# Attention chunks of 32 tokens on eight TensorE tiles, instead of 64 tokens on four, in an RWKV-6 and MLP-mixer kernel

## The chip, the cores and the metric

The kernel runs on one core of a Trainium2 chip. The metric is device time in microseconds (us), the median of several executions. The span that a profile shows is some 2 us shorter than the device time of the same execution; the kernel before was profiled in an execution of 687.6 us, at the fast end of its times. PE is TensorE, DVE is VectorE, ACT is ScalarE. Intervals of ratios are 95%; behind a median stand the lowest and the highest time.

## The reference, cut to what matters

```python
# attention, batch 4, 8 heads, 768 tokens, head size 48, fp32
for t in range(S):
    cur = einsum('bhd,bhe->bhde', u * k[t], v[t])
    y[t] = einsum('bhd,bhde->bhe', r[t], state + cur)
    state = w[t][..., None] * state + einsum('bhd,bhe->bhde', k[t], v[t])
# then, on x = y laid out as (batch, 768, 384): token mixing, channel mixing
u = x + (relu(x.T @ w_tok1) @ w_tok2).T
out = u + relu(u @ w_ch1) @ w_ch2
```

The four mixing weights arrive in a 64-bit form and are converted on the chip, in 28 pieces.

## The kernel before

The recurrence is computed in chunks. A *unit* is 256 tokens of one batch for all heads; three units make a batch, twelve the problem. Inside a chunk of `T = 64` tokens the products of r and k are built level by level: at level l, blocks of 2^l tokens are joined, so 64 tokens need a first block and levels 1 to 5 (`LEVELS = 6` in all). Each level is a *gram* on PE, a masked copy of its result out of PSUM, where PE's results lie in this kernel, on DVE (for the upper levels a plain copy on ACT), and a scaling of k and r by decay products on DVE.

```python
def gram(l):                       # 8 pieces x 4 tiles = 32 fp32 matmuls
    ...
    for ca in range(UC * A):
        fours(lambda q, j, rows, cols: pe.matmul(
            g[cols, q, ts(ca, 32)], k_[rows, ds(ca * 128 + j * T, T)],
            right[rows, ts(2 * ca + j, 32 // b), :], start=True, stop=True))

def block(l):
    gram(l)
    join(l, products[l], products[l + 1])      # DVE: scales k and r, next decay product
    pick(l)                                    # DVE or ACT: masked copy out of PSUM

def carry(c):                      # k^T v of each chunk, then the state, chunk by chunk
    ...
        dve.tensor_mul(new, state[bt, g], L["w"][:, c, :, j].unsqueeze(2).to_broadcast([128, A, D]))
        dve.tensor_add(new, new, got)

def before(c): ...                 # y  = r @ state      (PE, tile row q, tile column j)
def within(c):                     # y += at @ v         (PE)
    ...
            pe.matmul(y[ts(j, T), q, ts(a, D)], at[ts(j, T), q, c * A + a, :],
                      vt[ts(j, T), c, ts(2 * a + q, D)], ...)   # tile row j, column j: the diagonal
```

The program is emitted in an order that weaves lists of pieces by weight; the compiler's scheduler then reorders inside what the dependences allow. Batch 0 has no mixing work to weave with its attention: its units 0 to 2 form the head of the program, together with the weight conversions. The attention of batch n+1 is woven with the mixing of batch n.

```python
emit(woven(levels(0), levels(1)))
emit(woven(levels(2), p0 + p1, to_tok1))           # p0, p1: the rest of units 0 and 1
...                                                # conversions woven with batch 0's mixing
emit(woven(att, pieces))                           # batch n+1's attention with batch n's mixing
```

## Time and profile before

| | before |
|---|---|
| median of 4 executions | 692.76 us (689.45 to 696.67) |
| span of the profiled execution | 685.6 us |
| PE instructions (a load or a matmul each) | 17,168 |
| first "back" matmul (second half of token mixing) of batches 0 to 3 | 85.3, 268.0, 423.0, 575.9 us |
| last weight conversion ends | 183.9 us |

The row of "back" matmuls is the ruler: they split a span into the head (to 85.3), batch 0's mixing with batch 1's attention (182.7), two dense batches (155.0 and 152.9) and the tail (109.7). The five sum to the span.

### The profile page before, as it was taken

The numbers are of one execution on the slowest core, as the hardware profiler recorded it, in microseconds if no ns is written. First come the engines' busy times: TensorE is split into PE (matmuls) and PEld (weight loads), VectorE is DVE, ScalarE is ACT, GpSimd is POOL, SyncE is SP. The second block draws the span as 40 slices with busy tenths as digits, with TensorE's granted clock in tenths as the row PEclk, the third lists the DMA queues.
The fourth block names the chain that finished last, engine by engine and source line by source line (L and its number), as shares of the span: only waits on it lengthen the run. The fifth ranks groups of instructions, "written<-read, shape, count | busy, mean of one in ns | idle before, by whom it ended". The sixth has DMA issues, their size and how long they took to land.

```text
span 685.6 us, 18835 instructions
## 1 busy us (share of the span) xinstructions
PE 641.6 (94%) x8584; PEld 466.9 (68%) x8584; DVE 293.1 (43%) x585; ACT 194.8 (28%) x489; POOL 7.2 (1%) x32
## 2 busy tenths in 40 slices
PE   3889998996799999999999999999999999999998
PEld 3877656863586666788677656788677655786854
DVE  5998899998821435442242305442132211000000
ACT  7144533441242123432321303432211201220200
POOL 3000000000000000000000000000000000000000
PEclk9997898998899999999999999999999999999999
DMA  9244544332202131110210312000000000000000
GB/s 345 69 107 132 146 140 126 124 115 71 70 25 81 36 95 48 25 25 5 80 35 3 94 35 60 2 2 2 13 13 2 25 12 12 1 0 12 12 16 31
DMA packets 16111, 38.56 MB, mean 56 GB/s; under 512 B 2176, under 2 KB 8320, under 8 KB 16032
## 3 DMA queue, kind: packets, MB, share of 16 engines
q1 hardware_dynamic: 15888, 37.36, 17.9%
q8 instruction: 67, 1.10, 0.7%
q14 instruction: 12, 0.10, 0.0%
q10 hardware_dynamic: 144, 0.00, 0.0%
HBM read 32.64 MB, written 4.72 MB: 54 GB/s over the span
## 4 chain that ended last, share of the span: by engine, by line
PE 87%; DVE 9%; issue 2%; ACT 1%; DMA 1%; SPq 0%; DVEq 0%; ACTq 0%
PE z_ps L375 29%; PE h_ps L384 28%; PE gram L225 9%; PE h_ps L353 5%; PE h_ps L360 5%; PE y_ps L331 4%; PE kv_ps L296 2%; PE y_ps L318 2%; DVE r L251 1%; DVE k L250 1%; PE kT_ps L284 1%; PE gram L211 1%; PE xT_ps L367 1%; DVE at L217 1%; DMA w<-in_rkw_dram 1%
## 5 line engine op out<-in xcount | busy, mean ns | idle before, releaser
L375 PE MATMUL z_ps<-xT,wch 128*128 128x256 f32 x864 | 203.2, 389 | 3.5 <-DVE wch L161 3.0
L384 PE MATMUL h_ps<-wch,z 128*128 128x384 f32 x576 | 198.6, 498 | 3.7 <-DVE wch L161 3.5
L375 PEld LDWEIGHTS z_ps<-xT,wch 128*128 128x128 f32 x864 | 161.4, 192 | 28.4 <-DVE wch L161 3.2
L384 PEld LDWEIGHTS h_ps<-wch,z 128*128 128x128 f32 x576 | 107.9, 192 | 73.1 <-DVE wch L161 3.7
L377 ACT ACTIVATE z<-z_ps 128x256 f32<-128x256 f32 x144 | 55.1, 383 | 177.3 <-PE z_ps L375 177.2
L225 PEld LDWEIGHTS gram<-r,k 48*64 48x64 f32 x3840 | 76.5, 152 | 34.7 <-issue 24.3
L225 PE MATMUL gram<-r,k 48*64 48x32 f32 x3840 | 85.2, 235 | 13.1 <-DVE r L251 8.5
L388 DVE TENSOR_TENSOR o<-x,h_ps 128x384 f32<-128x384 f32 x24 | 13.3, 554 | 181.9 <-PE h_ps L384 181.9
L250 DVE TENSOR_TENSOR k<-k,decay 112x512 f32<-112x512 f32 x36 | 24.9, 691 | 62.2 <-PE gram L225 62.2
L242 ACT COPY at<-gram 16x256 f32<-16x256 f32 (+1 forms) x72 | 31.2, 434 | 44.7 <-PE gram L225 37.3
L250 DVE TENSOR_TENSOR k<-k,w 112x512 f32<-112x512 f32 x36 | 24.8, 688 | 39.6 <-PE gram L225 32.9
L360 PE MATMUL h_ps<-h,wtok 128*128 128x384 f32 x96 | 36.0, 503 | 1.8 <-DVE x L362 1.8
L353 PE MATMUL h_ps<-x,wtok 128*128 128x384 f32 x96 | 37.0, 520 | 0.0
L331 PEld LDWEIGHTS y_ps<-vt,at 64*64 64x64 f32 x768 | 26.2, 142 | 9.9 <-ACT seen L324 6.3
L234 DVE COPY_PREDICATED at<-mask,gram 128x512 f32<-128x512 uint8 x36 | 32.3, 897 | 0.0
L251 DVE TENSOR_TENSOR r<-r,w 112x512 f32<-112x512 f32 x36 | 24.7, 686 | 16.5 <-ACT rp L195 16.5
L331 PE MATMUL y_ps<-vt,at 64*64 64x48 f32 x768 | 29.2, 227 | 2.1 <-ACT seen L324 1.8
L211 PE MATMUL gram<-rp,kp 48*64 48x64 f32 x768 | 20.1, 246 | 11.1 <-ACT kp L199 8.0
L211 PEld LDWEIGHTS gram<-rp,kp 48*64 48x64 f32 x768 | 17.1, 154 | 16.4 <-ACT kp L199 10.4
L217 DVE COPY_PREDICATED at<-mask,gram 128x512 f32<-128x512 uint8 x24 | 16.7, 725 | 25.7 <-PE gram L211 25.4
L155 ACT ACTIVATE size<-d 128x384 f32<-128x384 f32 (+1 forms) x28 | 17.0, 608 | 28.2 <-DMA d<-in_w_ch_dram 13.3
L324 ACT COPY seen<-y_ps 64x2 f32<-64x2 f32 x44 | 6.8, 154 | 63.6 <-PE y_ps L318 63.3
(50 smaller groups left out, 429.1 us busy)
## 6 DMA issues: line engine op xcount, KB each, us to landing
vt<-in_v_dram SPq DMA_DIRECT2D x12, 384.0 KB, 3.9
d<-in_w_ch_dram SPq DMA_DIRECT2D x9, 512.0 KB, 3.6
d<-in_w_ch_dram SPq DMA_DIRECT2D x12, 384.0 KB, 3.0
out_dram<-o SPq DMA_DIRECT2D x24, 192.0 KB, 1.9
w<-in_rkw_dram SPq DMA_DIRECT2D x18, 192.0 KB, 3.5
k<-in_rkw_dram SPq DMA_DIRECT2D x18, 192.0 KB, 3.5
r<-in_rkw_dram SPq DMA_DIRECT2D x18, 192.0 KB, 3.4
r<-in_rkw_dram SPq DMA_DIRECT2D x3, 512.0 KB, 6.1
```

The source lines that it names most:

```text
L211: pe.matmul(g[cols, q, ts(a, T)], L["kp"][rows, tokens], L["rp"][rows, tokens], start=True, stop=True)
L225: fours(lambda q, j, rows, cols: pe.matmul(g[cols, q, ts(ca, 32)], k_[rows, ds(ca * 128 + j * T, T)], right[rows, ts(2 * ca + j, 32 // b), ...
L234: dve.copy_predicated(out=dst, data=g.rearrange("p q (m b) -> p q m b", b=b), mask=masks[l].rearrange("p x t -> p (x t)").rearrange("p (m ...
L242: act.copy(at[p:p + b, :, :, n * 2 * b + b:(n + 1) * 2 * b], g[p:p + b, :, :, ts(n, b)])
L250: dve.tensor_mul(left, left, wv[:, :, 1].unsqueeze(2).to_broadcast([ROWS, n, b]))
L251: dve.tensor_mul(right, right, wv[:, :, 0].unsqueeze(2).to_broadcast([ROWS, n, b]))
L331: pe.matmul(y[ts(j, T), q, ts(a, D)], at[ts(j, T), q, c * A + a, :], vt[ts(j, T), c, ts(2 * a + q, D)], start=(2 * ch + j == 0 and a == A ...
L353: pe.matmul(sums[i], wtok1[:, c, ts(i, 128)], xs[bt][:, c, :], start=(c == 0), stop=(c == C - 1))
L360: pe.matmul(ps, wtok2[:, i, ts(c, 128)], h1[:, i, :], start=(i == 0), stop=(i == DTOK // 128 - 1))
L375: pe.matmul(ps, wch1[:, m, ts(jt, 128)], xT[:, m, ts(s, SEG)], start=(m == 0), stop=(m == DM // 128 - 1))
L377: act.activation(zs[s][:, jt, :], ps, AF.Relu)
L384: pe.matmul(ps, zs[s][:, jt, ts(n, 128)], wch2[:, jt, :], start=(jt == 0), stop=(jt == NJ - 1))
```

## The change

The intent: with 32-token chunks one level goes away, and every small product spreads over eight tiles of TensorE instead of four (or, in the product with V, two). Besides, the attention of batch 1 and its loads are fenced behind the last weight conversion (a fence is an added dependence: no instruction of them may run before it), so that DVE finishes the conversions sooner.

```diff
-T = 64
+T = 32
+J = 128 // T
-LEVELS = 6
+LEVELS = 5
+TILES = ((0, 0), (1, 1), (0, 2), (1, 3), (0, 1), (1, 0), (0, 3), (1, 2))
@@ gram
-                fours(lambda q, j, rows, cols: pe.matmul(
-                    g[cols, q, ts(ca, 32)], k_[rows, ds(ca * 128 + j * T, T)],
-                    right[rows, ts(2 * ca + j, 32 // b), :], start=True, stop=True))
+                for q, j in TILES:
+                    rows = slice(q * P, q * P + D)
+                    pe.matmul(g[ts(j, T), q, ts(ca, T // 2)], k_[rows, ds(ca * 128 + j * T, T)],
+                              right[rows, ts(J * ca + j, T // 2 // b), :], start=True, stop=True)
@@ the state, now a piece of its own
+                        for a in range(A):
+                            dve.scalar_tensor_tensor(new[:, a], state[bt, g][:, a], L["w"][:, c, a, j:j + 1], got[:, a],
+                                                     op0=ALU.mult, op1=ALU.add)
@@ the product with V: tile row j, tile column j ^ 2q
+                    pe.matmul(y[put(q, j), q, ts(ca, D)], at[ts(j, T), q, ca, :], vt[ts(j, T), c, ts(2 * a + q, D)], ...)
@@ the fence
+    def fenced(pieces):
+        def run(f):
+            done = len(block.instructions)
+            f()
+            for ins in block.instructions[done:]:
+                if ins.engine in last:      # last instruction of the conversions on that engine
+                    tc.add_manual_dep(ins, last[ins.engine], behind, reason="behind the conversions")
...
+            emit(fenced(loads))
-            emit(woven(att, pieces))
+            emit(woven(fenced(att) if bt == 0 else att, pieces))
```

(Cut: the gram buffer becomes single, the masked copy moves ahead of the scaling, masks are built for both sizes of T, V's product is copied out in three pieces.)

## The prediction

> **What bounds the kernel now.** I read the page first (busy shares, then the chain that ended last), then busy time by stretch, then the waits of the one stretch where TensorE is not busy, then TensorE's own timeline inside the small attention matmuls, and last the groups kept apart by shape.
>
> ```profile
> span 685.6 us, 18835 instructions
> PE 641.6 (94%) x8584; PEld 466.9 (68%) x8584; DVE 293.1 (43%) x585; ACT 194.8 (28%) x489; POOL 7.2 (1%) x32
> ...
> PE 87%; DVE 9%; issue 2%; ACT 1%; DMA 1%; SPq 0%; DVEq 0%; ACTq 0%
> ```
>
> TensorE carries 87% of the chain; nothing else is near its limit over the whole span. The stretches show that this is an average over two different stages:
>
> ```profile
> 130.00:147.00 17.00, 17.00 (x74) 12.92 (x72) 15.65 (x34) 6.63 (x16) 0.00 (x0) 1.00 0.42 121
> 147.00:187.00 40.00, 28.94 (x600) 18.86 (x600) 35.59 (x73) 8.99 (x19) 0.00 (x0) 0.87 0.25 74
> 187.00:685.00 498.00, 489.41 (x5687) 349.29 (x5685) 128.94 (x255) 121.81 (x315) 0.56 (x5) 1.00 0.10 28
> ```
>
> (Stretch, its length, busy time of PE, weight loads, DVE, ACT, POOL, then clock.) From 187 us on TensorE is busy 489 of 498 us at the full clock: every microsecond of PE work taken out there is a microsecond off the end. From 147 to 187 it is the reverse: DVE is busy 35.6 of 40, PE 28.9, and the clock drops to 0.87. The DVE timeline says why:
>
> ```profile
> 149.35 0.69 DVE L250 TENSOR_TENSOR k<-k,decay 112x512 f32<-112x512 f32 x1 [0.28 <-PE gram L225]
> 149.96 0.55 DVE L161 SCALAR_TENSOR_TENSOR wch<-size,scale 128x384 f32<-128x384 f32 x1
> 150.43 0.35 DVE L156 TENSOR_SCALAR cut<-d 128x384 uint32<-128x384 uint32 x1
> 150.69 0.68 DVE L251 TENSOR_TENSOR r<-r,decay 112x512 f32<-112x512 f32 x1
> 151.30 0.55 DVE L157 SCALAR_TENSOR_TENSOR cut<-d,cut 128x384 uint32<-128x384 uint32 x1
> ```
>
> The last weight conversions (L156 to L161) alternate with the attention of batch 1 (L250, L251, L217, L234), although the program emits the conversions first. One conversion took 3.1 us while it had DVE to itself (L161 ends of 133.6, 136.75, 139.85 us); here it takes 5 to 6. The last one ends at 183.9 us, and only from there is PE dense.
>
> How fast the small matmuls go is in the PE timeline:
>
> ```profile
> 301.50 1.13 PE L225 MATMUL gram<-r,k 48*64 48x32 f32 x64
> 302.57 0.48 PE L375 MATMUL z_ps<-xT,wch 128*128 128x256 f32 x1
> ...
> 315.99 1.14 PE L331 MATMUL y_ps<-vt,at 64*64 64x48 f32 x32
> 317.06 0.48 PE L375 MATMUL z_ps<-xT,wch 128*128 128x256 f32 x1
> ```
>
> 64 instructions in a gram (an fp32 matmul is two instructions) cost 1.07 us to the next big matmul, and only 32 in the product with V cost the same. The gram uses four tiles (two row groups by two columns), the V product only the two on the diagonal. In the single start times of the trace both repeat every 58.3 ns per tile, whatever streams (32 or 48 columns): the load of 64 weight columns sets the pace. Within one round, starts on different tiles are 6.7 ns apart, the same 6.7 in the low-clock part of the head, so that step belongs to issue and not to the array. About 0.93 us of the 1.07 is the matmuls, the rest is change of tiling.
>
> ```profile
> L252 DVE TENSOR_TENSOR w_chunk<-decay 112x16 f32<-112x16 f32 x12 | 2.0, 173 | 0.7
> L305 DVE TENSOR_TENSOR state<-state,w_chunk 128x192 f32<-128x192 f32 x40 | 14.2, 356 | 1.0
> L306 DVE TENSOR_TENSOR state<-state,kv_ps 128x192 f32<-128x192 f32 x40 | 14.1, 352 | 21.5 <-PE kv_ps L296 20.8
> L234 DVE COPY_PREDICATED at<-mask,gram 128x512 f32<-128x512 uint8 x36 | 32.3, 897 | 0.0
> L242 ACT COPY at<-gram 32x512 f32<-32x512 f32 x24 | 13.8, 576 | 19.4 <-PE gram L225 19.3
> ```
>
> [...]
>
> **The change part by part.** A unit is 256 tokens; there are 12, three for each batch.
>
> PE, per unit now: six grams of 64 instructions, 64 for the state products, 64 for R times state, 64 for the V product at half speed. Summing start-to-start times between 395 and 550 us (one batch), attention takes 38.5 us of PE, 12.8 per unit: grams 7.0, V product 2.0, state products 1.2, R times state 1.2, transposes 1.2 (rounded).
>
> After: five grams, since one level goes, but every product has 128 instructions, on eight tiles at once. Weights are 32 columns wide except in the state products. [...] Eight pairs at 6.7 ns need 53.3 ns, so issue and no longer the weight load is the bound: 16 rounds of 53.3 = 0.85 us for a product; 16 rounds of 58.3 = 0.93 for the state products with their 64-column weights. With 0.2 us for each change of tiling: grams 5 x 1.05 = 5.3, state products 1.1, R and V products 1.05 each, transposes 1.2: 9.7 us. That is 3.1 less per unit. Nine units lie after the last conversion: -28 us on the path.
>
> DVE, per unit: one level less of k and r scaling (start to start 0.60 each) and its decay product: -1.3. The first masked copy runs once instead of twice: -0.6; three masked copies have half the columns: -0.8. The state update turns from 8 operations of 0.27 into 32 of 48 elements. [...] independent small operations start about 0.12 us apart in this trace: 3.8 against 2.2 us, +1.6. Net -1.1 us a unit; after 187 us DVE is at 26%, so only the three units of the head count: -3, less about 1 for more mask casts at the start. The head's level chain of units 0 and 1, which runs at about 4.2 us a level for two units with PE at half clock (a gram 1.97 us), loses a level and half its PE time; most of that is DVE time already counted. I take -4 for the head in all.
>
> ACT: two 32-row copies of 0.58 us go in each unit, and the copies out of y cost three of 0.48 for two. It has room.
>
> The fence: 18 us of batch 1's DVE work before 184 us (unit 3 whole, the start of unit 4) moves behind the last conversion; start to start that is 16 us. The conversion ends at about 168 instead of 184. What moves still costs PE, about seven grams or 7.5 us: -8.5 net. Against it stands a restart: loads are also held (3.5 us to landing), then ACT prepares kp and rp (two 0.66 and eight 0.40, 4.6 us) before the first gram, and single-buffered grams chain PE to DVE. PE has 48 us of batch-0 mixing to fill this. I charge +5.
>
> Sum: 691 - 28 - 8.5 - 4 + 5 = 655.5 us.
>
> **The rivals.**
> 1. Issue is slower than 6.7 ns per pair. The steady rounds never went below 14.6 ns per pair, so no line proves that loads and matmuls can be fed at 6.7 each for 128 pairs; in a warm round four loads start and then four matmuls, 6.7 apart. If each instruction takes its own 6.7 ns, a pair takes 13.3 and a product 1.71 us: seven products longer by 0.86, +6 us a unit, +54 on nine: about 709. For the faster case: at a burst's start four loads and four matmuls come in pairs within one 6.7 ns step, and in the low-clock head a load and a matmul start 2 ns apart. In between, at 8.3 ns, +1.5 us a unit: about 669.
> 2. A wait takes the place. One gram buffer instead of two and 32 dependent state updates before R times state: where the woven mixing between them is shorter than the DVE work, PE stops. In the dense stage about 10 us of mixing lies there against some 7 of DVE work; in batch 0's tail less. A microsecond or two a unit: 665 to 673.
> 3. The fence gives back what it gains (the restart costs 10 to 15 us of PE): about 663.
> 4. Faster than issue-bound [...]: about 640; the 6.7 ns steps speak against it.
>
> **Range and chances.** Most weight lies on the first working (655), with rivals 2, 3 and the middle form of 1 all pulling up; I put the prediction at 658. Low end 638: issue-bound with no restart cost and a better head. High end 692: half of the slow form of 1. Faster by over 2% (below 677): 0.73. Within 2%: 0.15. Slower (above 705): 0.12, the slow form of 1.
>
> **What would show it right or wrong.** Starts in an 8-tile gram 6.7 ns apart in the mean, a gram of 128 near 0.85 us and about 1.05 to the next big matmul (1.7 or more is rival 1). The last L161-type operation near 168 us with none of batch 1's attention before it. DVE after it well under half. PE idle after the last conversion below 10 us, not tied to the state update (rival 2) or to kp, rp and the loads (rival 3). PE attention of 9 to 10 us a unit between 395 and 550 us. If the kernel is slower, I expect the single rate of eight-tile pairs to be the wrong term.

## The result, and the profile after

| | before | changed |
|---|---|---|
| median of 4 executions | 692.76 us | 729.34 us (727.12 to 730.12) |
| ratio | | 1.052 (1.046 to 1.059): slower |
| span of the profiled execution | 685.6 us | 727.8 us |
| PE instructions | 17,168 | 27,920 |
| first "back" of batches 0 to 3 | 85.3, 268.0, 423.0, 575.9 | 114.6, 310.0, 468.1, 618.3 |
| stretches: head, batch 1, dense, dense, tail | 85.3, 182.7, 155.0, 152.9, 109.7 | 114.6, 195.4, 158.1, 150.3, 109.5 |
| last weight conversion ends | 183.9 us | 176.8 us |

A ratio is the mean time of one kernel's fast runs over that of the other's of the same rounds, so it is not quite the ratio of the medians. The spans are 42.2 us apart, the medians 36.6, because the kernel before was profiled in a fast execution.

The "back" matmuls of the two kernels, before and changed (count, durations in ns, first and last start in us):

```profile
L360 PE MATMUL h_ps<-h,wtok x96: 486/486/590, 85.3 to 587.5; 128*128 128x384 f32 x96
```

```profile
L382 PE MATMUL h_ps<-h,wtok x96: 486/486/591, 114.6 to 629.8; 128*128 128x384 f32 x96
```

The page of the changed kernel, to set against the first fence of the prediction:

```profile
span 727.8 us, 29744 instructions
PE 633.9 (87%) x13960; PEld 460.0 (63%) x13960; DVE 300.4 (41%) x818; ACT 180.4 (25%) x446; POOL 6.5 (1%) x32
...
PE 77%; DVE 10%; issue 9%; DMA 2%; ACT 1%; SPq 0%; DVEq 0%; ACTq 0%
```

PE is busy for 8 us *less* than before in a span 42 us longer. What has grown in the chain is "issue", time in which the engine waits for nothing that the profile shows: 2% before, 9% now. The waits say where it sits (engine and line, what it waited for, us in total, times, longest):

```profile
PEld gram L242 <- issue: 50.9, 54, 4.2
...
PE gram L242 <- issue: 33.8, 20, 4.1
```

So the grams stand still for up to 4 us at a time, and no semaphore holds them. The stretches (in the form of the prediction) locate the loss. Before, the head and one dense batch:

```profile
0.00:85.00 85.00, 66.19 (x1862) 56.18 (x1862) 69.89 (x147) 39.75 (x100) 6.66 (x27) 0.92 0.50 160
...
268.00:423.00 155.00, 153.99 (x2154) 110.63 (x2146) 53.05 (x102) 44.52 (x115) 0.22 (x2) 1.00 0.15 40
```

Changed, the same two:

```profile
0.00:115.00 115.00, 61.75 (x3090) 47.57 (x3090) 82.06 (x228) 32.17 (x75) 5.90 (x27) 0.91 0.31 105
...
310.00:468.00 158.00, 151.06 (x3494) 109.70 (x3490) 53.06 (x158) 40.81 (x104) 0.25 (x2) 0.99 0.15 40
```

The head has 66% more matmuls, less PE busy time, and takes 30 us longer. The dense batch has 62% more matmuls and takes 3 us longer. The two dense batches together are 308.4 us against 307.9: nothing gained, nothing lost. Of the 42.2 us, 29.3 are lost in the head and 12.7 in the stretch with batch 1's attention. (The clock column is too high for the head: the profile has no clock record before 41.7 us in the kernel before and before 79.7 us in the changed one, and the first record is each time a rise to the full clock. A gram before that takes 1.97 us in the kernel before, 1.06 in its dense batches. So PE probably ran at half clock until then, twice as long in the changed kernel; but since PE is busy for less time there than before, that alone does not make the loss.)

What a pause looks like, in the chain inside the head of the changed kernel (start, length, what):

```profile
22.94 1.12 PE gram L242 x66
24.06 1.07 issue
25.13 0.57 PE gram L242 x34
...
25.72 0.73 DVE at L250
...
26.50 1.12 PE gram L242 x67
27.63 0.96 issue
28.59 0.57 PE gram L242 x34
```

Every gram is cut at about the same place, a pause of a microsecond, then its rest. (The chain's counts leave out some matmuls.) Counting PE's instructions in the trace shows what the place is: in the head most pauses come 255 or 256 instructions apart. A gram of 64 fp32 matmuls is 256 instructions (two weight loads and two matmuls each), so each holds one such boundary. The view of DMA queues has a partner for it, the queue that carries instructions. Before, and changed:

```profile
q8 instruction: 67, 1.10, 0.7%
```

```profile
q8 instruction: 109, 1.79, 1.1%
```

(Packets, MB, share.) 1.79 MB over 109 is 16 KB a packet, and 109 packets of 256 are 27,904, PE's 27,920 instructions but for a rest; in the kernel before 67 of 256 are 17,152 of 17,168. So this queue feeds PE, by division 64 bytes an instruction. Single packets can be set against the pauses. In the pause at 24 us above, the stream had entered its present 256 instructions at 21.58 us; a packet started at 22.78, ended at 23.71, and PE ran on at 25.13: 1.2 us to the packet's start, 0.93 for it, 1.42 from its end to the first instruction, 3.55 in all. The trace of the changed kernel has 32 pauses of PE above 0.7 us before an instruction that waits on no semaphore; all 32 end 1.25 to 1.56 us after the last packet has ended, in 30 of the 31 steps from one to the next the count of instructions is within 6 of a multiple of 256, and they sum to 62.8 us: 30.3 before the first "back" matmul, 21.6 before the second, 11.0 later. No two packets of this queue start less than 3.31 us apart in the trace of the changed kernel, 3.38 in that of the kernel before. The kernel before has one such pause at a boundary (1.2 us at 18 us).

That gives the theory F: PE's instructions arrive in blocks of 256 (109 packets for 27,920), a block runs no earlier than about 3.5 us after the one before it was entered (3.55 in the pause above), and the changed kernel runs through 256 instructions in 1.1 us at the full clock (1.6 in the head) wherever nothing slow is woven in. The rivals: R1, the fence; R2, array time; R3, DVE's state update and the single gram buffer; R4, a cost of 32-token chunks in every unit alike.

### The profile page after: what moved, and what is told of

Same layout as the page of the kernel before. It is cut to its first block, busy times and chain, and to the rows that moved or that the text cites. A ratio compares the mean times of both kernels' runs of the same rounds, so it can differ in the third digit from the quotient of the medians.

```text
span 727.8 us, 29744 instructions
## 1 busy us (share of the span) xinstructions
PE 633.9 (87%) x13960; PEld 460.0 (63%) x13960; DVE 300.4 (41%) x818; ACT 180.4 (25%) x446; POOL 6.5 (1%) x32
## 3 DMA queue, kind: packets, MB, share of 16 engines
q8 instruction: 109, 1.79, 1.1%
## 4 chain that ended last, share of the span: by engine, by line
PE 77%; DVE 10%; issue 9%; DMA 2%; ACT 1%; SPq 0%; DVEq 0%; ACTq 0%
PE h_ps L406 25%; PE z_ps L397 23%; PE gram L242 8%; PE h_ps L375 5%; PE h_ps L382 4%; PE kv_ps L308 3%; PE y_ps L355 3%; PE y_ps L342 2%; PE kT_ps L296 2%; PE gram L228 2%; DVE wch L183 1%; DVE scale L181 1%; DVE scale L182 1%; DVE cut L179 1%; DVE state L326 1%
## 5 line engine op out<-in xcount | busy, mean ns | idle before, releaser
L242 PE MATMUL gram<-r,k 48*32 48x16 f32 x6144 | 67.5, 196 | 41.2 <-issue 33.8
L242 PEld LDWEIGHTS gram<-r,k 48*32 48x32 f32 x6144 | 59.9, 116 | 61.9 <-issue 50.9
L326 DVE SCALAR_TENSOR_TENSOR state<-state,w_chunk,kv_ps 128x48 f32<-128x48 f32 x352 | 63.3, 259 | 19.9 <-PE kv_ps L308 19.8
L250 DVE COPY_PREDICATED at<-mask,gram 128x256 f32<-128x256 uint8 x36 | 19.0, 529 | 68.6 <-PE gram L242 68.6
L257 ACT COPY at<-gram 16x256 f32<-16x256 f32 x48 | 17.4, 362 | 68.3 <-PE gram L242 67.9
L228 PE MATMUL gram<-rp,kp 48*32 48x32 f32 x1536 | 18.3, 215 | 17.0 <-ACT kp L221 7.5
L355 PE MATMUL y_ps<-vt,at 32*32 32x48 f32 x1536 | 20.2, 229 | 14.0 <-issue 12.6
L355 PEld LDWEIGHTS y_ps<-vt,at 32*32 32x32 f32 x1536 | 16.8, 114 | 19.0 <-issue 16.6
L375 PEld LDWEIGHTS h_ps<-x,wtok 128*128 128x128 f32 x96 | 19.2, 213 | 13.4 <-issue 3.0
L233 DVE COPY_PREDICATED at<-mask,gram 128x512 f32<-128x512 uint8 x12 | 8.8, 732 | 45.1 <-PE gram L228 45.1
```

The costliest lines, as they stand in the source:

```text
L228: pe.matmul(g[ts(j, T), q, ts(ca, T)], L["kp"][rows, tokens], L["rp"][rows, tokens], start=True, stop=True)
L242: pe.matmul(g[ts(j, T), q, ts(ca, T // 2)], k_[rows, ds(ca * 128 + j * T, T)], right[rows, ts(J * ca + j, T // 2 // b), :], start=True, st ...
L326: dve.scalar_tensor_tensor(new[:, a], state[bt, g][:, a], L["w"][:, c, a, j:j + 1], got[:, a], op0=ALU.mult, op1=ALU.add)
L355: pe.matmul(y[put(q, j), q, ts(ca, D)], at[ts(j, T), q, ca, :], vt[ts(j, T), c, ts(2 * a + q, D)], start=False, stop=ca == 0, skip_group_c ...
L375: pe.matmul(sums[i], wtok1[:, c, ts(i, 128)], xs[bt][:, c, :], start=(c == 0), stop=(c == C - 1))
```

## The experiments

Fifteen kernels ran, all correct within the reference's tolerance. The table gives the ruler for each; the texts below quote what was expected before each ran.

| run | ratio to before | head | batch 1 | dense, dense | instruction packets in head, batch 1 |
|---|---|---|---|---|---|
| before | 1 | 85.3 | 182.7 | 155.0, 152.9 | 14, 17 |
| changed | 1.052 | 114.6 | 195.4 | 158.1, 150.3 | 24, 29 |
| 64 tokens, fence | 1.004 | 90.1 | 186.8 | 155.0, 152.9 | 13, 18 |
| 64 tokens, fence, early loads | 0.999 | 88.0 | 185.2 | 155.0, 152.9 | 13, 18 |
| changed, no fence | 1.046 | 123.6 | 182.1 | 156.6, 148.8 | 26, 27 |
| 64 tokens, extra matmuls in head | 1.051 | 115.2 | 193.6 | 155.0, 152.9 | 23, 17 |
| 64 tokens, extra matmuls in units 6 to 11 | 1.045 | 85.1 | 191.8 | 166.4, 166.7 | 14, 18 |
| changed, half instructions in units 0 to 2 | 1.011 | 77.0 | 205.3 | 158.4, 147.2 | 12, 29 |
| the same, grams and state products twice | 1.037 | 105.7 | 188.3 | 156.8, 151.1 | 21, 28 |
| changed, half instructions in units 0 to 5 | 0.955 | 77.5 | 166.5 | 157.3, 146.4 | 12, 17 |
| the same, twice in units 3 to 5 | 0.998 | 77.2 | 193.5 | 158.7, 147.2 | 12, 26 |
| 64 tokens in batch 0, then 32 | 1.008 | 90.5 | 194.3 | 149.8, 153.2 | 14, 28 |
| changed, state update in two operations | 1.054 | 124.1 | 182.9 | 158.9, 150.0 | 24, 29 |
| 64 tokens, half instructions in units 0 to 2 | 1.017 | 75.4 | 205.1 | 155.0, 152.9 | 7, 17 |
| 64 tokens, V on four tiles, everywhere | 0.996 | 88.9 | 188.4 | 152.3, 150.2 | 14, 17 |
| ... in units 3 to 11 | 0.990 | 85.3 | 186.9 | 152.3, 150.2 | 14, 17 |
| ... in units 6 to 11 | 0.998 | 87.3 | 182.5 | 152.3, 150.2 | 14, 17 |

How far the ruler can be trusted: each row is one execution. The run with extra matmuls in units 6 to 11 shows it. Up to 262 us of the kernel before, the two execute the same DVE and ACT instructions in the same order (375 and 230), and yet batch 1's stretch differs by 9.1 us. The granted clock does: PE was at half clock for 10 us between 150 and 200 us in the kernel before and for 31 in the other. First the kernel before, then that run (the clock is the third number from the end):

```profile
150.00:200.00 50.00, 39.12 (x640) 27.85 (x642) 34.85 (x74) 12.20 (x28) 0.00 (x0) 0.90 0.22 63
```

```profile
150.00:200.00 50.00, 39.30 (x574) 26.88 (x568) 34.21 (x71) 10.71 (x25) 0.00 (x0) 0.69 0.19 57
```

So a difference of up to 9 us in the column "batch 1" can be the clock of that one execution. In the 64-token runs the dense columns repeat to 0.1 us where the edit leaves them alone.

### The fence, alone and taken away

On the kernel before, the fence and the held loads alone:

```diff
+    loads = [f for p in (p0, p1, p2) for f in p[-2:]]
...
             emit(woven(downs[0][:-4], to_ch2[6:]))
+            emit(fenced(loads))
-            emit(woven(att, pieces))
+            emit(woven(fenced(att) if bt == 0 else att, pieces))
```

> The kernel before (64-token chunks) with the fence and the held loads alone. Theory F (the loss comes from TensorE's instruction stream: every 256 of its instructions need a fetch that takes about 3.55 us from the moment the stream enters a block to the moment the next one can run, and the changed kernel has 60% more of them): the fence is harmless or a small gain, 680 to 690 us, the last conversion ends near 165 to 170 us. Rival R1 (the fence makes the loss, by holding batch 1's attention back): 700 us or more.

Measured: 695.33 us, ratio 1.004 (1.001 to 1.008). The last conversion did end at 163.3 us instead of 183.9, as the fence intends, and yet the second "back" came at 276.9 instead of 268.0. F's numbers missed too (a gain or nothing was expected). Where the 20 us went is in two stretches of that run:

```profile
90.00:163.00 73.00, 59.02 (x231) 40.91 (x230) 65.95 (x127) 25.06 (x58) 0.00 (x0) 1.00 0.42 130
163.00:277.00 114.00, 103.35 (x2045) 74.43 (x2046) 55.41 (x108) 39.45 (x105) 0.34 (x3) 0.94 0.33 85
```

Before 163 us PE now runs only 231 matmuls and idles 14 of 73 us (the kernel before runs 1,011 from 85 to 184 us), since the attention that used to stand there is held. Behind it all of batch 1's attention has to be done, and PE idles another 11 of 114 us. The fence moved PE work from a stretch with idle time to a stretch that sets the end.

The changed kernel without it:

```diff
-    loads = [p.pop() for p in (p0, p1, p2)]
-            emit(fenced(loads))
-            emit(woven(fenced(att) if bt == 0 else att, pieces))
+            emit(woven(att, pieces))
```

> The changed kernel (32-token chunks) without the fence, loads back in their old place. Theory F: still slow, 722 to 740 us, first token mixing done near 114 us as with the fence. Rival R1 (the fence makes the loss): 690 to 700 us.

Measured: 723.53 us, ratio 1.046 (1.042 to 1.050). Still slow, so R1 is not the main cause; the fence costs the changed kernel about 0.6% at most (1.052 against 1.046, from different rounds, with intervals that overlap). Its first token mixing was done at 123.6 us, 9 later than I expected, with the next stretch shorter for it; its pauses before that, counted as above, sum to 39.3 us instead of 30.3.

With the attention fenced but the loads in their old place:

> The kernel before with the fence on batch 1's attention but its loads left in their old place. With both held, the last conversion ended 20.7 us earlier and the kernel was 0.4% slower. If the held loads are what gave the gain back (they land behind the fence while TensorE waits): ratio 0.98 to 0.993. If it is the late start of the attention itself, or the head's changed order: 0.997 or more.

Measured: 692.36 us, ratio 0.999 (0.994 to 1.004). The held loads are at most the 3 us between these two runs; the gain does not come back without them. So it is the late start of the attention, or the changed order in the head (88.0 and 90.1 us against 85.3), which I did not separate.

### More instructions in the kernel before

In units 0 to 2 each gram gets a second set of small matmuls into unused PSUM columns:

```diff
+            if i < 3:
+                for ca in range(UC * A):
+                    fours(lambda q, j, rows, cols: pe.matmul(
+                        g[j * T:j * T + 40, q, ds(256 + ca * 4, 4)], k_[rows, ds(ca * 128 + j * T, 40)],
+                        r_[rows, ds(ca * 128 + j * T, 4)], start=True, stop=True))
```

> The kernel before with as many TensorE instructions in the first three units as the changed kernel has there: each gram gets a second set of matmuls of 40 weight columns and 4 streamed columns into unused PSUM columns (the result stays right). 448 more pairs a unit, 2688 more instructions, 10.5 more blocks of 256. Theory F: 10.5 blocks at 3.55 us are 37 us of fetching, of which most shows: the first token mixing is done at 105 to 120 us instead of 85, total 710 to 730 us, with pauses at every 256th instruction. Rival R2 (array time or VectorE makes the loss, not the count): the extra array work is about 0.6 us a gram, 13 us in all, mostly in the head's idle time: 691 to 700 us.

Measured: 727.74 us, ratio 1.051 (1.048 to 1.054); first "back" at 115.2 us. That is the loss of the changed kernel, on 64-token chunks, four tiles, and VectorE work untouched. (I had counted seven grams a unit; there are six. The trace has 2,304 instructions more, 9 packets: 19,472 against 17,168 and 76 against 67. F's 3.55 us for each would be 32 us; the head grew by 29.9.) But it is not as clean as I had meant it: in the head the added matmuls of one gram take about 1.24 us (0.76 and 0.48 around the pause in the chain), twice my 0.6. Over 18 grams that could be 22 us of array time. The pauses at the 256th instruction are there, 19 us of them in the head, but this run alone does not separate F from R2.

The same edit with `i >= 6`, in the dense batches:

> The same extra matmuls as in the head run, but in units 6 to 11, woven with dense mixing: 5376 more instructions, 21 blocks of 256. If each block cost what it did in the head (36 us over 10.5 blocks): 72 us more, 764 us. Theory F with fetching hidden behind the mixing's slow matmuls: only the array time of the extra pairs, 0.45 to 0.65 us a gram, 42 grams, 19 to 27 us: 711 to 720 us.

Measured: 723.72 us, ratio 1.045 (1.038 to 1.051). The dense batches grew by 11.4 and 13.8 us. There are 36 grams and 18 blocks here, not 42 and 21 (21,776 instructions, 85 packets). A gram takes 1.67 us to the next matmul instead of 1.06, which makes 22 us of array time over 36; pauses of the kind above come to 3 us. So 18 more blocks of instructions cost at most some 3 us of their own where slow mixing matmuls lie between the bursts, where 9 had cost the head 30 us together with their array time. (The total is a few us above the range; the stretch of batch 1, untouched by the edit, came out 9 us longer than in the kernel before, by the clock as told above.)

### Fewer instructions in the changed kernel

A matmul of two fp32 operands is two load-and-matmul pairs here (128 in the trace for the 64 calls of a gram). If the operands are read as bf16, the upper halves of the same words, it is one pair (64 in the trace). This is less exact on purpose, and it changes nothing outside PE:

```diff
+    def top(t, n):
+        return t.bitcast(mybir.dt.bfloat16).rearrange("p (n two) -> p n two", two=2)[:, :, 1] if n < 3 else t
...
-                    pe.matmul(g[ts(j, T), q, ts(ca, T // 2)], k_[rows, ds(ca * 128 + j * T, T)],
+                    pe.matmul(g[ts(j, T), q, ts(ca, T // 2)], top(k_, i)[rows, ds(ca * 128 + j * T, T)],
```

> The changed kernel with the TensorE operands of units 0 to 2 read as bf16 (the upper halves of the same fp32 words; a less exact result on purpose): the same matmuls on the same tiles, but one instruction pair each instead of two, so 512 pairs a unit instead of 1024. VectorE, ScalarE, buffers and the fence are untouched. Theory F (instruction fetch bounds the head): first token mixing done at 82 to 95 us instead of 114, total 694 to 710 us. Rival R3 (the single gram buffer and the longer state update on VectorE slow the head): stays above 105 us there and above 718 in total.

Measured: 700.66 us, ratio 1.011 (1.006 to 1.017). The head falls from 114.6 to 77.0 us, with the fence, the single gram buffer and the state update as they were: R3 is out as the cause of the head's loss. The array time saved is more than the 0.5 us a product of a dense batch: in the timelines of the head a gram of the changed kernel runs 1.12 and 0.50 us around its pause, one of the half run 0.66. Over 24 products that could be 23 us, and the head fell by 37.6; the pauses in it (over 0.7 us, no semaphore, ending 1.2 to 1.6 us after a packet) fell from 30.3 us to 1.7. The chain in the head shows what bounds it then:

```profile
33.90 0.60 DVE r L270
34.50 0.61 DVE scale L181
35.14 0.70 DVE scale L182
...
38.59 4.87 DVE state L330 x28
```

DVE work end to end, with no pause. Then, to bring the count back at a small and known array time, the grams and state products of the same kernel are issued twice, the second overwriting the first with the same values:

```diff
-                for q, j in TILES:
+                for q, j in TILES * (2 if i < 3 else 1):
```

> The changed kernel with bf16 reads in units 0 to 2, as in the half-head run, but there each gram and state-product matmul is issued twice (the second overwrites the first with the same values): 384 pairs a unit come back, 896 instead of 512. By the rate seen in undisturbed bursts, 8.3 ns a pair, their array time is 3.2 us a unit, 9.6 in all. Theory F: 9 blocks more in the head at 3.55 us each, first token mixing done at 97 to 112 us (77 in the half-head run, 114.6 in the changed kernel). If array time and not the count matters: 77 to 87 us.

Measured: 717.37 us, ratio 1.037 (1.030 to 1.044); first "back" at 105.7 us, in the range F gave and 19 us above the other. These lines of the two runs give the ruler (count, durations in ns, first and last start in us), first the half run, then the doubled one:

```profile
L388 PE MATMUL h_ps<-h,wtok x96: 486/486/590, 77.0 to 599.3; 128*128 128x384 f32 x96
```

```profile
L388 PE MATMUL h_ps<-h,wtok x96: 486/486/590, 105.7 to 613.3; 128*128 128x384 f32 x96
```

And the chain in the head of the doubled run has the pauses back, where DVE had been end to end:

```profile
33.79 0.91 PE gram L246 x89
34.70 2.66 issue
37.36 0.47 PE gram L246 x30
```

Nine blocks more (21 packets against 12) cost 28.7 us, 3.2 each. The doubled pairs themselves take at most 11 us (1,152 pairs at the 9.7 ns that the undisturbed part of a head gram shows), while the pauses in the head, counted as before, rise from 1.7 us to 32.6. This pair of runs is the one that separates F from R2.

The half run left 205.3 us in the stretch of batch 1. With bf16 reads in units 0 to 5:

> The changed kernel with bf16 reads in units 0 to 5, so that batch 1's attention also has half the TensorE instructions. Theory F says that the loss left after the head was mended (205 us from the first token mixing's end to the second's, 183 in the kernel before) is fetching again, 29 blocks there against 17: at most 192 us in that stretch, total 680 to 692 us. Rival R1 in its small form (batch 1's late start behind the fence sets that stretch): 200 us or more, total above 695 us.

Measured: 659.09 us, ratio 0.955 (0.951 to 0.960). The stretch fell to 166.5 us, the fence still in place, so the fence does not set it. The total is far below the range that I gave, and I had not counted that three units' array time on the path is halved too, some 13 us. As a kernel it is no fair rival of the others, since its attention in half the units is less exact; as an experiment it says that the 32-token program is fast when half its units have half the PE instructions and half the array time.

With the doubled grams in units 3 to 5:

> bf16 reads in units 0 to 5 with the doubled grams and state products in units 3 to 5 only. The stretch from the first to the second token mixing was 166.5 us with half the instructions there and 205 with all of them. Theory F: 183 to 198 us. Array time alone (9.6 us at 8.3 ns a pair): 168 to 177 us.

Measured: 692.52 us, ratio 0.998 (0.992 to 1.004); the stretch rose from 166.5 to 193.5 us, 27 us for nine packets more, where array time alone gives at most 11. The pauses grow by 10 us, and the granted clock between 175 and 200 us is 0.80 instead of 1.00. So the same waits are in batch 1's stretch too, where three units' attention has only some 48 us of woven mixing. How much of the 12.7 us lost there is theirs stays open, since the clock alone moved that stretch by 9.

### 64 tokens in the head, 32 later

Both versions of the attention in one kernel, chosen by unit, without the fence. Space had to be found: one output buffer and two state buffers fewer, and grams of batch 0 alternate between two PSUM tiles.

```diff
+    def levels(i):
+        return levels64(i) if i < 3 else levels32(i)
```

> 64-token chunks for batch 0 (units 0 to 2), 32-token chunks for the nine other units, no fence. Theory F: the head is as before (85 to 90 us), the dense batches are as in the changed kernel (157 and 150 us), total 688 to 702 us. Rival R4 (32-token chunks cost about the same in every unit): three of twelve units saved, 715 to 722 us.

Measured: 699.12 us, ratio 1.008 (1.002 to 1.014). The head is back at 90.5 us and the dense batches are 149.8 and 153.2, as F says; R4 is out. What remains is batch 1's stretch, 194.3 us.

### The state update

In the changed kernel, two operations of 192 elements in place of four of 48:

```diff
-                        for a in range(A):
-                            dve.scalar_tensor_tensor(new[:, a], state[bt, g][:, a], L["w"][:, c, a, j:j + 1], got[:, a], ...)
+                        dve.tensor_mul(new, state[bt, g], L["w"][:, c, :, j].unsqueeze(2).to_broadcast([128, A, D]))
+                        dve.tensor_add(new, new, got)
```

> The changed kernel with its state update as two operations of 192 elements a chunk instead of four of 48: 16 operations of about 0.27 us a unit in place of 32 of about 0.18. Theory F: VectorE has room, 724 to 733 us. Rival R3 (the state update on VectorE paces the loss): 718 us or less.

Measured: 728.29 us, ratio 1.054 (1.049 to 1.060). No gain, R3 is out here as well. (The head was 9.5 us later and the next stretch 12.5 shorter than in the changed kernel; I do not know why.)

### The head of the kernel before

The bf16 reading in units 0 to 2 of the 64-token kernel (the same helper, all five products):

> The kernel before with bf16 reads in units 0 to 2 (a less exact result on purpose): half the TensorE instructions in its own head. Theory F taken to its end says that the kernel before waits for instructions too when it runs two units' levels alone (256 instructions a level, 4.2 us): first token mixing done at 72 to 80 us instead of 85, total 677 to 687 us. If VectorE alone bounds that head: 84 us or more, total 689 to 694 us.

Measured: 701.77 us, ratio 1.017 (1.013 to 1.022): *slower*, by 1.7%, and my total was wrong. The head came out as F said, 75.4 us instead of 85.3. But that does not show that the kernel before had been waiting for instructions there: its head has one pause of the kind above, 1.2 us, and the other grams in its chain run through without one, at the slow pace of that part, the 64 pairs of a gram in 1.97 us:

```profile
27.46 1.97 PE gram L225 x64
```

Half the array time is the likelier cause. The 10 us were then more than given back: the last conversion ended at 200.2 us and the second "back" came at 280.5. The stretch before that shows PE at half clock:

```profile
175.00:200.00 25.00, 18.82 (x271) 11.78 (x270) 16.86 (x37) 3.49 (x8) 0.00 (x0) 0.50 0.18 49
```

Conversions and batch 1's attention alternate there as in the kernel before, for 16 us longer. In this execution PE was at half clock from 162.6 to 203.5 us without a break, for 9 us in that time in the kernel before. All four executions had a low mean clock (0.942 to 0.946), so it is not chance; what brings it about is open.

### A version that beats both

The one idea of the change that costs no instructions is to use more tiles in the product with V. On 64-token chunks, half q of the heads and half j of the tokens go to output half j ^ q, four tiles instead of two, and the copy out of PSUM puts them right:

```diff
+        def put(q, j):
+            return ts(j ^ q if i >= 3 else j, T)
-                    pe.matmul(y[ts(j, T), q, ts(a, D)], at[ts(j, T), q, c * A + a, :],
+                    pe.matmul(y[put(q, j), q, ts(a, D)], at[ts(j, T), q, c * A + a, :],
...
+            act.copy(x[:, 0], got[:, 0])
+            for n in range(2):
+                act.copy(x[ts(n, P), 1], got[ts(1 - n, P), 1])
```

First in every unit (the cut above is of the later run, from unit 3 on):

> The kernel before with the V product on four tiles instead of the two of the diagonal (token half j of head half q goes to output half j xor q, and the copy out of PSUM puts it right). The count of TensorE instructions is unchanged. If tiles run side by side there as in the gram, each of 24 V products falls from 0.93 to 0.47 us, 8 to 11 us in all: 680 to 684 us. If something else paces it: 689 to 693 us.

Measured: 688.98 us, ratio 0.996 (0.994 to 0.999), a third of what was expected. The product itself did what it should, 32 instructions in 0.61 us to the next matmul where the prediction's fence shows 1.07 (this from the run from unit 3 on):

```profile
320.21 0.68 PE L335 MATMUL y_ps<-vt,at 64*64 64x48 f32 x32
320.82 0.92 PE L385 MATMUL z_ps<-xT,wch 128*128 128x256 f32 x3
```

and each dense batch gained 2.7 us, but the head lost 3.6 and the stretch after it 5.7 (its clock between 150 and 200 us was 0.73, against 0.90 before). So it was kept out of the head:

> The kernel before with the V product on four tiles in units 3 to 11 only, so that the head is untouched. The run with it everywhere gained 2.7 us in each of the two dense batches and lost 3.6 and 5.7 in the head and behind it. If those losses come from the head's schedule: 682 to 687 us. If the four-tile product itself costs later work: 688 us or more.

Measured: 685.25 us, ratio 0.990 (0.984 to 0.995). With the next one this is the fastest exact kernel, though 1% is inside the 2% that count as the same here. Batch 1's stretch is still 4 us longer than before, and the clock there is 0.73 again, so that this difference says nothing about the edit. From unit 6 on:

> The kernel before with the four-tile V product in units 6 to 11 alone, the two dense batches, so that nothing before 268 us changes. If the 4 us lost behind the head in the run from unit 3 came from the order of work around the last conversions: 2 x 2.7 us gained and nothing lost, 684 to 688 us, ratio 0.990 to 0.994. If the ratio is 0.996 or more, the gain in the dense batches is given back.

Measured: 687.64 us, ratio 0.998 (0.993 to 1.004), which does not tell it from the kernel before, though its profiled execution (682.0 us) has the 5.4 us of the two dense batches. By its text this falls on the "given back" side; by its ruler it does not. The list of executions settles it for the ruler. The six fall into two groups: 683.95 to 684.72 us at a mean granted clock of 0.980 to 0.982, and 690.55 to 693.37 at 0.960 to 0.965. Of the kernel before, in the same rounds, seven ran at 0.980 to 0.983, with a median of 689.67 us (685.15 to 691.4), and one at 0.963 (693.43); three more at 0.966 to 0.970 (696.15 to 699.95) were slow and left out of the ratio. At the same high clock the version is about 5 us faster, what its two dense batches gained, and the run from unit 3 on is its equal there (684.05 to 684.82 at 0.980).

## Why the prediction was wrong, point by point

The bound was read rightly: PE carries the chain, the dense stage is full of it, the head is not. The step that failed is the one that PE's time in a burst is issue plus array, "eight pairs at 6.7 ns need 53.3 ns, so issue and no longer the weight load is the bound". That 32 columns load in less than this was my estimate. Above that step stands another: in the head 256 instructions took about 3.5 us to arrive (3.55 in the pause told above), 27 ns for each of 128 pairs, and the head came out 29.3 us longer where 4 were to be gained. The prediction counted instructions only to multiply them by a pace in the array, and never asked how they get to PE. The row of instructions in the page (17,168 for PE) and the queue of instruction packets were both before me. The kernel before has one pause of this kind (1.2 us at 18 us), and I read past it.

Term by term, in the order of the sum 691 - 28 - 8.5 - 4 + 5:

- **PE in nine units, -28.** The mean pace of a pair on eight tiles was 8.5 ns in the grams (8.3 in their steady rounds), 9.2 in the R and V products and 10.4 in the state products, not 6.7. Eight pairs at 8.5 ns are 68 ns for a round of the eight tiles, though the weights have half the columns, against 58.3 for a round of four before. On four tiles a narrower load did go with a faster pace: the added 64 pairs of a gram in the run with extra matmuls in units 6 to 11 (40 weight columns) took 0.61 us where the gram's own 64 (64 columns) took 1.06, though fewer columns stream there too (4 against 32). The change of tiling shows in both traces: a 256-column matmul is followed by its like after 216 ns and by the first of a gram after 309. An undisturbed gram of 128 pairs takes 1.19 us to the next big matmul, not 1.05:

```profile
363.23 1.26 PE L242 MATMUL gram<-r,k 48*32 48x16 f32 x128
364.42 1.56 PE L397 MATMUL z_ps<-xT,wch 128*128 128x256 f32 x6
```

  The R and V products took 1.30 instead of 1.05, the state products with 64-column loads 1.47 instead of 1.1. In all that is 1.6 us a unit, 14 us of the 28 over nine units. In the six units of the two dense batches the measured sum is +0.5 us with 11.0 us of pauses in it; if the pauses are taken off in full, which is an estimate, it would be -10.5, 1.75 a unit instead of 3.1. So the mechanism (fewer levels, full tiles) was right, its size about half, and even in the dense batches fetching took the rest.
- **The head, -4.** It became +29.3. This is the largest miss. With half the instructions it ends at 77.0 us, 8 less than before; but PE's array time is halved there too, so no run shows the DVE saving by itself.
- **The fence, -8.5, and the restart, +5.** The last conversion ended at 176.8 us (168 was predicted); with the fence alone at 163.3, so the reading that batch 1's attention delays the conversions was right. But alone it was a loss of 0.4% in a kernel otherwise unchanged, not a gain of 3.5 us: PE idles while it is held, and the work comes later on the path.
- **DVE.** A state update took about 0.175 us start to start, 5.6 us a unit, where I had 0.12 and 3.8; a single one lasts 259 ns. The two-operation run shows that this cost nothing at the end.
- **Rival 1** named slower issue as the likeliest way to be wrong, and gave 709 us for it; but as a constant price for each pair, which the dense batches refute. Its middle form, 8.3 ns and 669 us, had the pace of a burst about right, and missed the wait between bursts as the first working did. **Rival 2**, waits on the single gram buffer or the state: the half run refutes it in the head. **Rival 3**, the fence gives its gain back: yes, and a little more.
- **The list of signs** said that PE idle after the last conversion should stay below 10 us and not be tied to state or loads. It was 35 us, and most of it tied to neither: the pauses make 32.6. "issue" was not on the list.

## What to carry to other kernels

Count a program's PE instructions and where they bunch, not only their array time: in the head of the changed kernel a run of several hundred short matmuls with nothing slow woven between was paced by the arrival of its instructions, 256 in some 3.5 us. A smaller tile that does the same work in twice the instructions cost little more than its array time here where long matmuls lie between (3 us over 18 blocks in one run, 11 us of pauses in the dense batches of the changed kernel), and was dear where PE runs through attention alone (28.7 us for nine blocks in the head of the doubled run). And when a profile says "issue", compare the places of the pauses with the instruction count and with the instruction queue before looking for a wait. Before two single profiles are compared, compare their granted clocks, stretch by stretch.
